# Fused attention and channel mixing on one core: q of batches 3 and 4 turned by the DMA crossbar, and the sums and outputs of two head groups in one TensorE block

## The chip, the cores and the metric

The kernel runs on one core of a Trainium2 chip. The metric is device microseconds of one execution; the time before is the median of three runs, 195.05 us (194.85 to 195.09). The profile is that of one execution, traced by the hardware profiler. Engines: PE is TensorE's matmul, PEld its weight load, DVE is VectorE, ACT is ScalarE, POOL is GpSimd and SP is SyncE, which only issues DMAs here.

## The reference

There are 8 batches, 8 heads, 576 positions and a head size of 64. An attention without a score matrix comes first, then a channel mixing over rows of 512 (8 heads x 64):

```python
q_s = softmax of q over the head dimension          # row sums, then a scale
k_s = softmax of k over the sequence                # column sums
kv  = einsum('bhsd,bhse->bhde', k_s, v)            # 64 x 64 per head
x   = q_s @ kv, heads side by side                  # 576 x 512 per batch
xk  = mu_k * x + (1 - mu_k) * x_prev                # x_prev: the row before
xr  = mu_r * x + (1 - mu_r) * x_prev
k   = relu(xk @ w_k); v = k * k @ w_v               # 512 -> 1024 -> 512
out = sigmoid(xr @ w_r) * v
```

## The kernel before

**Attention.** Work goes by batch b (0 to 7) and head group g (0 and 1), four heads each; a name's digits are b and g (expq30: batch 3, group 0). ScalarE takes exponentials of q and k (expq, expk) and casts v (cast). VectorE sums the rows of q (rsum), inverts (rrec) and scales (scale). For a matmul q must stand with the head dimension on partitions. In batches 0 to 4 TensorE turns it: transposes of 64 rows into a PSUM tile, 18 instructions in the groups of WHOLE and 36 in the others, and ScalarE copies the result out (qt). In batches 5 to 7 (CROSSBAR) SP issues a transposing DMA from SBUF to SBUF instead, also named qt.

The sums k_s' v (kv, 36 matmuls of 64x65, whose last column is the sum of k) go to PSUM. VectorE inverts the sum (rz) and scales the 64x64 blocks (w). The outputs x are matmuls of w with the turned q: four of 64 columns (the last 64 positions) and four of 512 columns. ScalarE copies them to SBUF (xs the 64 columns, xb the 512), VectorE fixes the edge (edge), takes the difference to the row before (diff), scales it by mu (sc, four per group) and adds (mix). A name mix300 is batch 3, group 0, and a last 0 for xk or 1 for xr. Batch 0 and some of batch 1 are done in finer pieces.

**Blocks on TensorE.** From batch 1 on, the transposes and sums of one group are one block, together with the outputs of a group before it: TKV10, TKV20 and TKV30 have no outputs, B11, B21, B31, B40, ..., B71 have those of an earlier group, and X11, X21 and X71 are outputs alone (ALONE). A block with sums takes one of two att tiles (two PSUM banks each) for its sums, its transposed q and the 64 output columns (column offsets KVO and XO), and the other for the 512 output columns.

**Channel mixing.** The 4608 rows go in ten units of 512 or 256 columns (k0 to k9). For each there are eight k (four matmuls of 128x512, then relu on ScalarE and a square sq on VectorE), and for each tile of 128 rows an r (four matmuls, then tanh th on ScalarE) and a v (eight matmuls, then o on VectorE: (1 + tanh) times v), and the stores st on SP. k, r and v share four PSUM banks (mm 0 to 3). k22 is unit 2, eighth 2; r30 is unit 3, tile 0; v210 and v211 are the first and second half of unit 2, tile 1. A k may start when mix of its columns is there: unit 2 needs batch 2, units 3 and 4 need batch 3, unit 5 batch 4.

**Order.** The order is written out as a list of names (ORDER) with the buffer number behind a colon. Each engine gets its part of the list in this sequence and works it off strictly in order; waits follow from the data. POOL issues the loads and weights, in list order and with no more than eight on the way. Around the lines that the prediction speaks of, TensorE's part of the list before is

```
TKV10:1 r02:2 r01:1 r00:3 r03:0 B11:0.1 ... X21:0.1 v111 v101 r20:0 TKV30:1 v130:2 v131 k22:0
k20:1 k24:3 k23:0 k21:2 k27:3 B31:0.1 k25:1 k26:2 r22:0 r30:3 B40:1.0 r23:0 v220:2 v200:1
```

and POOL's first loads are load00v, load01v, load10q0, wk00, load10q1, load11q0, wk01, load10k0, wk10, wk11, load10k1, load10v0, load10v1, load11q1, wr.

Of the kernel before, what the change touches and what calls it, by code (L numbers as in the profile page):

```python
# [39 lines left out]
ALONE = ((1, 1), (2, 1), (B - 1, 1))  # L40
CROSSBAR = tuple((b, g) for b in range(5, B) for g in range(2))
# [16 lines left out]
x0111 sq03 k05:1 expk101 x0110 cast100:0 load11k0:9 cast101 load11k1 relu04:0 expq111 load11v1
k07:0 sq02 relu05:1 sq01 k06:3 wv0 rrec100 rrec110 scale100 sq04 TKV10:1 rz10:2 w10:0 relu06:2
wv1 sq06 rsum111 qt10:2 r02:2 r01:1 relu07:0 r00:3 cast110:1 expk110:0 expk111 rrec111 cast111  # L60
r03:0 scale111:0 scale110 wv2 wv3 B11:0.1 load30q0:10 rz11:0 th00:0 th03:1 w11:1 sq07 th02:2
xb10:0 v030:3 xs10 qt11:0 v000:0 sq05 edge10 th01:3 v010:2 diff10:0 sc1001:0 v011 v001 v031
sc1000 load20q0:0 X11:1.0 xs11:1 load20v0:2 sc1011:1 v012 v020:1 v021 xb110 sc1010 v013 v032
load21q0:1 xb111 edge11 v002 v003 v033 v022 load20k0:3 mix100 diff110:1 diff111 sc1100:2 o01
sc1111:0 expq300:1 v023 sc1101 expq200:0 mix1100 k11:2 load21k0:4 cast200:2 o00 mix1101 sc1110
load21v0:6 load31q0:7 k11.2 o03 k10:0 k11.3 load31v0:5 relu11:2 load30k0:9 expq210:2 k10.2
load50v0:8 k10.3 rsum200:0 o02 st03.2 k17:3 k12:2 relu17:0 relu10:1 k12.2 expk200:1 k12.3
rrec200 mix101 load31k0:10 load30v0:0 k13:1 k13.2 sq11:1 k13.3 relu12:2 scale200:1 sq10 mix111
sq12 k16:3 expk210:2 st02.2 k15:0 relu16:1 rsum210:1 relu15:2 TKV20:0 st00 sq16 cast210:0 r10:2
rz20:1 r11:3 k14:0 rrec210 relu13:1 sq17 w20:2 load40q0:2 th11:4 qt20:1 r12:1 r13:3 relu14:0  # L70
scale210:2 expq310:0 st03 rsum300:3 th12:5 th13:6 sq14 sq13 load40v0:1 B21:1.0 sq15 rz21:2
xb20:0 v120:0 v100:1 v110:3 st01 w21:0 xs20 st02 rrec300 rsum310:2 scale300:0 load40k0:3
load50k0:4 qt21:2 v121 X21:0.1 expk300:0 edge20 rrec310 diff20:0 v111 xs21:1 xb21 v101 o12
cast300:1 r20:0 sc2001:2 th10:1 TKV30:1 edge21 v130:2 diff21:1 sc2000 expq400:2 th20:2 sc2101:1
sc2011:0 mix200 rz30:0 load51k0:6 sc2100 v131 w30:1 expk310:1 cast310:2 st12.2 mix210 k22:0 o10
o11 load60q0:7 load41v0:9 relu22:0 st00.2 st12 qt30:0 k20:1 o13 st13.2 k24:3 relu24:1 relu20:2
k23:0 load50q0:0 k21:2 k27:3 load71k0:2 cast400:0 load51q0:10 scale310:1 rsum400:0 sq24:0 sq20
relu21:1 relu23:2 B31:0.1 sc2010 sc2111:2 mix201 rrec400 load41k0:5 k25:1 rz31:1 sq23 sc2110
w31:2 k26:2 expk400:2 xb30:0 mix211 xs30 scale400:2 relu27:2 r22:0 qt31:1 edge30 sq21 sq27 sq22
th22:0 r30:3 B40:1.0 diff30:0 rz40:2 sc3000:1 relu26:1 relu25:2 xb31:1 xs31 sc3001 th30:5  # L80
load41q0:1 expq500:1 st11 edge31 sq26 expq510:0 sq25 st10.2 load51v0:3 r23:0 mix300 diff31:1
v220:2 expk500:0 v200:1 v201 st01.2 sc3101:0 st10 th23:3 v230:3 v221 st13 st11.2 o20 sc3100 v231
mix310 k45:1 sc3011:2 o22 k40:0 o23 st22 sc3010 sc3110:1 expq410:2 relu45:0 cast410:1 k43:2
sc3111 k42:1 st20.2 relu43:1 sq45:1 relu40:2 relu42:0 r21:3 v210:2 load70v0:0 w40:0 qt40:2
load70q0:10 rsum410:1 load70k0:4 sq40 k30:0 rrec410 load60k0:1 k41:1 v211 relu30:2 mix311 sq43
k37:0 load61q0:9 scale410:0 th21:1 k33:3 o21 cast500:2 expk410:1 k46:2 sq30:0 sq42 mix301
relu37:1 relu41:2 st20 B41:0.1 rsum500:3 rz41:0 k34:0 relu33:0 sq41 sq37 k47:1 xb40:1 sq33 xs40
relu47:2 rrec500 w41:1 rsum510:2 relu46:1 scale500:1 relu34:0 load61k0:8 sq34 qt41:0 load60v0:5
st22.2 r40:3 k31:1 st23 sq47 k32:2 th40:6 r41:0 B50:1.0 relu32:0 rrec510 relu31:2 expk510:2
r31:3 th31:4 k44:2 r33:1 st21 sq46 edge40 th41:2 relu44:1 diff40:0 k36:3 sc4000:0 cast600:0  # L90
xs41:0 sq32 v400:0 scale510:2 sq44 xb41 st23.2 qt50:1 th33:0 expk610:1 sc4001 mix400 rz50:1
v410:2 qt51:2 v401 load71q0:6 v411 sq31 relu36:0 cast510:1 sc4010:1 edge41 sc4011 expq600:2
diff41:1 k35:1 mix401 v330:3 w50:2 o40 sc4100:2 o41 sc4101 v300:0 mix410 relu35:1 k57:2 sq36
expq710:1 k51:1 relu57:2 B51:0.1 sc4111:0 rsum600:0 sq57:1 rrec600 relu51:0 k55:2 xb50:1 sq35
xs50 relu55:2 sc4110 v331 sq51 v301 load61v0:5 load71v0:8 mix411 v310:1 rz51:2 st41.2 scale600:0
expq610:0 expk600:0 o30 sq55 st41 expq700:2 r51:2 o33 edge50 st33.2 k54:0 k56:3 v311 relu54:1
rsum610:1 w51:0 expk700:2 diff50:0 sc5000:1 st30 st30.2 st33 B60:1.0 sc5001 o31 r50:0 qt60:0
rsum710:3 sq54 xs51:0 rsum700:2 k50:1 th51:3 xb51 edge51 relu50:0 relu56:2 sq56 r32:2 st31.2
th32:2 st21.2 sq50 diff51:1 mix500 sc5100:2 rrec710 v320:1 v321 sc5101 mix510 o32 rz60:0 k52:3
sc5010:0 w60:1 cast710:2 th50:5 k53:2 relu52:1 sq52 sc5110:1 rrec610 sc5111 cast610:1 relu53:2  # L100
r53:0 r52:3 sq53 cast700:0 k61:1 relu61:0 st40.2 k67:2 scale610:1 k65:1 relu67:1 st32.2 sc5011
k63:2 qt61:1 th53:0 v530:0 relu65:2 rrec700 th52:1 sq67:0 B61:0.1 mix511 v500:1 v531 sq65 xs60:0
sq61 mix501 xb60 v501 scale700:2 k62:3 relu62:1 expk710:0 o53 edge60 k66:0 relu66:2 st53.2 st31
relu63:0 diff60:1 v510:3 sc6000:2 o50 rz61:1 w61:2 B70:1.0 v511 sc6011:1 scale710:0 v520:1
xb61:1 k64:0 v521 xs61 o51 sc6001 edge61 diff61:0 sc6100:0 rz70:2 st53 r63:2 qt70:2 mix600
th63:0 sq66 r61:3 relu64:2 w70:0 sc6101 B71:0.1 sq63 sc6010 mix601 k60:2 mix610 rz71:0 k73:0
sq64 w71:1 th61:4 relu60:0 sq60 st50.2 k76:3 o52 st50 sq62 r62:2 relu73:2 xb70:0 xs70 v620:0
relu76:0 k71:1 v621 qt71:0 k74:3 sc6110:2 relu71:1 sq73:1 st40 sc6111 mix611 edge70 sq76 th62:5
X71:1.0 relu74:2 v610:1 v611 xb71:1 k70:2 diff70:1 sc7001:1 xs71 o62 k77:0 edge71 relu70:0 k72:3
st62 r73:2 sq70 relu77:0 sq71 relu72:1 k75:0 o61 diff71:0 sq74 sc7101:0 th73:6 st62.2 r60:1  # L110
v630:3 v600:2 sq77 sc7000 sc7110:2 sc7100 mix710 st51.2 sc7011:0 th60:5 st52.2 relu75:2 v631
# [72 lines left out]
def graph(kn):  # L184
# [135 lines left out]
    def attention(b, g):  # L320
# [127 lines left out]
        else:  # L448
# [3 lines left out]
            def block():  # L452
                if crossed:
                    kv(qtp)
# [418 lines left out]
```

## Time and profile before

| | |
|---|---|
| median of 3 runs | 195.05 us (194.85 to 195.09) |
| profiled execution | 194.93 us, span 193.2 us |
| TensorE matmul busy | 185.2 us in 1830 matmuls |
| VectorE busy | 152.7 us |
| ScalarE busy | 138.6 us |
| GpSimd busy (DMA issue) | 41.4 us |
| read and written in HBM | 33.56 MB and 9.44 MB |

The span runs from the first instruction to the last; the rest of the execution's time lies around it. The page gives busy shares by engine and by slice, and the chain that ended last, followed back from the end. The windows give busy time of each engine in a stretch. Durations of instructions in the timeline overlap on an engine, since the next one starts while one drains, so what an instruction costs its engine is the distance from its start to the next start.

### The profile page before, as it was taken

The page shows a single profiled execution, that of the slowest core. Times are in us where ns is not written, and L with a number is a line of the kernel's source. Part 1 is how long each engine was busy: PE and PEld are TensorE (multiplying, and loading weights), DVE is VectorE, ACT ScalarE, POOL GpSimd, SP SyncE. Part 2 cuts the span into 40 slices and gives each one's busy share as a digit, 9 for nine tenths or more (in the row PEclk, how much of TensorE's full clock was granted, in tenths as well). Part 3 has the DMA queues.
Part 4 walks back from the last instruction along what each step waited for, and adds up shares of the span by engine and source line. Part 5 has one row for each costly group of instructions (what it writes and reads, how often), then busy time and mean ns, then how long its engine had stood idle before and what let it go on. Part 6 is the DMA issues. An engine that isn't in the chain of part 4 may idle for free.

```text
span 193.2 us, 4660 instructions
## 1 busy us (share of the span) xinstructions
PE 185.2 (96%) x1830; PEld 89.2 (46%) x1830; DVE 152.7 (79%) x355; ACT 138.6 (72%) x219; POOL 41.4 (21%) x65
## 2 busy tenths in 40 slices
PE   7798979999999999999999999999999999999991
PEld 2264434444535544654444444444444444444751
DVE  1898974999999999999999999998966863232531
ACT  3777999889999999898999798653754236421440
POOL 8345656544225114320210000000000000000000
PEclk9999999999999999999999999999999999999999
DMA  6999999999999999997692371459014145024813
GB/s 192 312 319 248 327 331 246 404 393 399 410 396 397 403 412 376 362 380 275 132 311 105 92 159 27 64 113 169 8 30 107 31 109 136 0 54 110 191 30 109
DMA packets 23615, 41.86 MB, mean 217 GB/s; under 512 B 9373, under 2 KB 12713, under 8 KB 23593
## 3 DMA queue, kind: packets, MB, share of 16 engines
q0 software_dynamic: 9392, 27.99, 43.6%
q1 hardware_dynamic: 13384, 12.14, 25.3%
q10 hardware_dynamic: 816, 1.44, 2.3%
q8 instruction: 14, 0.23, 0.5%
q14 instruction: 9, 0.07, 0.1%
HBM read 33.56 MB, written 9.44 MB: 223 GB/s over the span
## 4 chain that ended last, share of the span: by engine, by line
PE 84%; DMA 11%; POOL 2%; issue 0%; DVE 0%; POOLq 0%
PE mm_d L695 10%; PE mm_b L695 9%; PE mm_a L639 8%; PE mm_c L639 7%; PE mm_b L639 7%; PE mm_c L695 7%; PE mm_a L695 7%; DMA wk_ab<-in_moe_w_k_dram 7%; PE mm_d L639 6%; PE mm_c L675 5%; PE mm_d L675 5%; DMA wr<-in_moe_w_r_dram 4%; PE mm_a L675 4%; PE mm_b L675 3%; PE att_a L401 1%; PE att_b L543 1%
## 5 line engine op out<-in xcount | busy, mean ns | idle before, releaser
L695 PEld LDWEIGHTS <-k_a 128*128 128x128 bf16 x160 | 15.4, 98 | 18.5 <-issue 0.6
L675 PEld LDWEIGHTS <-xr 128*128 128x128 bf16 x144 | 13.6, 98 | 16.8 <-DMA wr<-in_moe_w_r_dram 1.3
L695 PEld LDWEIGHTS <-k_b 128*128 128x128 bf16 x136 | 12.9, 98 | 14.2 <-issue 0.8
L639 PEld LDWEIGHTS <-wk_ab 128*128 128x128 bf16 x80 | 7.8, 98 | 8.1 <-issue 0.5
L639 PEld LDWEIGHTS <-wk_aa 128*128 128x128 bf16 x80 | 7.6, 98 | 8.2 <-issue 0.7
L639 PEld LDWEIGHTS <-wk_bb 128*128 128x128 bf16 x80 | 7.8, 98 | 7.7
L675 PE MATMUL mm_c<-wr,xr 128*128 128x512 bf16 x40 | 10.3, 380 | 1.1 <-DMA wr<-in_moe_w_r_dram 1.1
L639 PEld LDWEIGHTS <-wk_ba 128*128 128x128 bf16 x80 | 7.5, 98 | 8.3 <-issue 0.7
L675 PE MATMUL mm_d<-wr,xr 128*128 128x512 bf16 x40 | 10.3, 379 | 0.0
L675 PE MATMUL mm_a<-wr,xr 128*128 128x512 bf16 x36 | 9.3, 380 | 0.0
L626 ACT ACTIVATE rel_a<-mm_b 128x512 bf16<-128x512 f32 (+1 forms) x7 | 3.6, 508 | 7.5 <-PE mm_b L639 7.2
L626 ACT ACTIVATE rel_c<-mm_a 128x512 bf16<-128x512 f32 (+1 forms) x11 | 6.1, 556 | 3.1 <-PE mm_a L639 2.8
L630 DVE TENSOR_TENSOR k_a<-rel_a 128x512 bf16<-128x512 bf16 x14 | 5.8, 418 | 3.1 <-ACT rel_a L626 2.9
L639 PE MATMUL mm_c<-xk,wk_ab 128*128 128x512 bf16 (+1 forms) x26 | 7.5, 362 | 0.2 <-ACT xk L503 0.2
L639 PE MATMUL mm_c<-xk,wk_aa 128*128 128x512 bf16 (+1 forms) x26 | 7.3, 363 | 0.0
L675 PE MATMUL mm_b<-wr,xr 128*128 128x512 bf16 x28 | 7.2, 379 | 0.0
L630 DVE TENSOR_TENSOR k_a<-rel_c 128x512 bf16<-128x512 bf16 x14 | 5.8, 414 | 1.7 <-ACT rel_c L626 1.7
L639 PE MATMUL mm_a<-xk,wk_ba 128*128 128x512 bf16 (+1 forms) x24 | 6.9, 371 | 0.0
L639 PE MATMUL mm_a<-xk,wk_bb 128*128 128x512 bf16 (+1 forms) x24 | 6.9, 370 | 0.0
L626 ACT ACTIVATE rel_a<-mm_c 128x512 bf16<-128x512 f32 x7 | 4.2, 602 | 3.3 <-PE mm_c L639 1.7
L639 PE MATMUL mm_b<-xk,wk_aa 128*128 128x512 bf16 (+1 forms) x24 | 6.5, 353 | 0.0
L639 PE MATMUL mm_b<-xk,wk_ab 128*128 128x512 bf16 (+1 forms) x24 | 6.5, 352 | 0.0
(344 smaller groups left out, 541.3 us busy)
## 6 DMA issues: line engine op xcount, KB each, us to landing
raw_k<-in_q_dram POOLq DMA_DIRECT2D x3, 576.0 KB, 8.4
raw_e<-in_k_dram POOLq DMA_DIRECT2D x3, 576.0 KB, 11.0
raw_f<-in_v_dram POOLq DMA_DIRECT2D x3, 576.0 KB, 6.8
out_dram<-th_a SPq DMA_DIRECT2D x13, 128.0 KB, 3.2
out_dram<-th_f SPq DMA_DIRECT2D x12, 128.0 KB, 2.4
out_dram<-th_b SPq DMA_DIRECT2D x10, 128.0 KB, 4.8
out_dram<-th_c SPq DMA_DIRECT2D x10, 128.0 KB, 2.4
raw_a<-in_q_dram POOLq DMA_DIRECT2D x2, 576.0 KB, 9.9
```

The costliest lines, as they stand in the source:

```text
L401: kn.nc.tensor.matmul(kn.half(slot, r)[two[u], KVO:KVO + n], lhsT=kn.eks[ek.index][two[r], j, u, :], rhs=by, start=(j == 0), stop=(j == J ...
L543: kn.nc.tensor.matmul(kn.half(slot, u)[two[r], to:to + n], lhsT=kn.ws[w.index][two[u], r, :], rhs=x_columns(r, u, at, n), start=True, stop ...
L626: kn.nc.scalar.activation(out=kn.rels[rel.index][:, 0:n], in_=kn.bank(kf)[:, 0:n], func=ACT.Relu, scale=HALF_ROOT)
L630: kn.nc.vector.tensor_tensor(out=kn.k2s[k2.index][:, fc, 0:n], in0=kn.rels[rel.index][:, 0:n], in1=kn.rels[rel.index][:, 0:n], op=ALU.mult)
L639: kn.nc.tensor.matmul(kn.bank(kf)[:, 0:n], lhsT=kn.wk[fc // 4][ct % 2][:, ct // 2, (fc % 4) * 128: (fc % 4) * 128 + 128], rhs=kn.xs[0][:, ...
L675: kn.nc.tensor.matmul(kn.bank(rps), lhsT=kn.xs[1][:, ct, c:c + 128], rhs=kn.wr[:, ct, :], start=(ct == 0), stop=(ct == CT - 1))
L695: kn.nc.tensor.matmul(kn.bank(vps)[:, 0:width], lhsT=kn.k2s[k2.index][:, ft, 128 * m:128 * m + 128], rhs=wv_of(ft)[:, part], start=(ft == ...
```

## The change

**Crossbar.** Batches 3 and 4 join the crossbar: their four TensorE transposes (18 instructions in group 30, 36 in 31, 40 and 41) and ScalarE's four copies qt30 to qt41 go, and SP issues four more transposing DMAs. The pool of turned q gets a fourth buffer. To make room, mu_rows lies in the last of the th buffers.

**Blocks.** For b = 3 to 8 a block M*b* takes the place of TKV30 and of B31 to B71 and X71. M*b* holds the sums of both groups of batch b (none for 8) and the outputs of both groups of batch b - 1 (none for M3, as batch 2's are done in B21 and X21). Its sums and 64-column outputs go to a new kind of PSUM place, duo: two of the four mm banks (0 and 1, or 2 and 3), at columns 0 and 72 for the sums and 144 and 216 for the outputs. The 512-column outputs of both groups take both att tiles. As the two banks of a duo are two tiles, there is no view over both: rz, w and xs become two instructions, one per bank.

**Order.** The whole list is new. TensorE's part around the lines of the prediction:

```
k00:2 k01:3 X010:1.0 k02:0 k03:1 k00.2 k02.2 k01.2 X011:0.1 k03.2 X001:0.3 mu:0 k05:1 k04:2 k07:3
TKV10:0 k06:1 r00:3 r01:2 r03:1 r02:0 B11:1.0 ... X21:1.0 r13:0 v100:1 v101 v130:3 v110:2 v131 v111
k22:1 k21:0 k20:1 k26:0 k24:1 k23:2 k27:3 k25:1 r23:0 M3:1 v230:1 v200:0 v201 v231 M4:1.1.0
r22:0 v220:1 v221 r21:2 r30:3 v210:0 v211 k31:2 k43:3 k47:1 ... M5:1.1.0 v401 v300:0 v301 r32:1
v320:2 v321 v330:3 v331 k50:1 ... M6:0.1.0 ... M7:1.1.0 ... M8:0.0.1 ... v831 r91:0 v900:3 v901
```

ScalarE's behind B11: th02 th03 xb10 xs10 th00 (before: th00 th03 th02 xb10 xs10). ScalarE's behind M4: xs31 xs30 xb30 xb31 expq510 th22 expk500 th21. VectorE's behind M3: rz30 rz31 sq27 w31 w30 scale400 o20 o23 rz41 rz40 w41 w40, and behind xb30: edge30 diff30 edge31, then sc and mix of batch 3. VectorE's last: o83 sq93 o90 o91 (before: sq90 to sq97 ahead of o90). SP's: st03 st00 st02 st00.2 st03.2 qt30 st01 st02.2 st12 qt31. POOL's first loads: load00v, load01v, wk00, load11q0, load10q0, load10q1, wk01, wk11, load10k1, wk10, load10k0, load10v0, load10v1, load11q1, wr.

The core of the diff:

```diff
-"qt": 3
+"qt": 4, ... "duo": 2
+          ("duo", 0): [("mm", 0), ("mm", 1)], ("duo", 1): [("mm", 2), ("mm", 3)]}
+KVM = (0, 72)
+XM = (144, 216)
-ALONE = ((1, 1), (2, 1), (B - 1, 1))
-CROSSBAR = tuple((b, g) for b in range(5, B) for g in range(2))
+ALONE = ((1, 1), (2, 1))
+CROSSBAR = tuple((b, g) for b in range(3, B) for g in range(2))
...
+        kvo = KVM[g] if crossed else KVO
...
-            def block():
-                if crossed:
-                    kv(qtp)
-                if turn_x:
-                    turn_x[0](qtp)
-                if not crossed:
-                    transpose_q(qtp)
-                    kv(qtp)
...
+            def copy_second(other, xo):
+                if kn.whole(other) is not None:
+                    kn.nc.scalar.copy(out=kn.xbs[xb.index][:, :, 576:640],
+                                      in_=kn.whole(other)[:, :, xo:xo + 64])
+                else:
+                    for u in range(2):
+                        kn.nc.scalar.copy(out=kn.xbs[xb.index][:, u, 576:640],
+                                          in_=kn.half(other, u)[:, xo:xo + 64])
...
+    def together(b):
+        groups = [attention(b, g) for g in range(2)] if b < B else []
+        turns, pending[:] = list(pending), []
+        duo = Slot("duo")
+
+        def block():
+            for kv, _, _, _ in groups:
+                kv(duo)
+            for turn, at in zip(turns, XM):
+                turn[0](duo, at)
+
+        m = add("PE", block, [o for t in groups for o in t[1]] + [o for t in turns for o in t[1]],
+                [duo] + [o for t in turns for o in t[2]],
+                [o for t in groups for o in t[2]] + [o for t in turns for o in t[3]], name=f"M{b}")
+        for turn, at in zip(turns, XM):
+            turn[4](m, duo, at)
+        for t in groups:
+            t[3](m, m, None, duo)
...
+    for b in range(B):
+        if (b, 0) in CROSSBAR:
+            together(b)
+        else:
+            for g in range(2):
+                attention(b, g)
+    together(B)
...
     def half(slot, i):
+        if slot.pool == "duo":
+            return ps["mm"][2 * slot.index + i][:]
...
-    kn.mu_rows = const.tile([2, 2, 256], F32, name="mu_rows")
+    kn.mu_rows = kn.ths[-1][0:2, :].rearrange("p (m c) -> p m c", m=2)
```

More of the change, by code (lines that the diff above doesn't have):

```diff
@@ L58 @@
[L58 to L63, printed above, removed]
@@ L70 @@
[L70 to L75, printed above, removed]
@@ L76 @@
[L76 to L93, printed above, removed]
@@ L106 @@
[L106 to L111, printed above, removed]
@@ L118 @@
[L118 to L121 removed]
+warm load00k1 load01v late load01k0:3 wk00 load11q0:4 load10q0:5 expq001:0 expq000 load10q1
+rsum001:0 ACT!load01k1 rsum000 wk01 expq011:1 rrec001 wk11 rrec000 rsum011:1 fill:1 fill.2:2
+fill.3:3 fill.4:0 fill.5:1 fill.6:2 fill.7:3 fill.8:0 fill.9:1 fill.10:2 fill.11:3 fill.12:0
@@ new lines @@
+cast400:0 sq27 w31:1 v201 cast410:1 w30:2 v231 expq410:1 scale400:2 load50k0:1 load71q0:4
+M4:1.1.0 load51v0:6 o20 o23 r22:0 xs31:1 v220:1 st11 st23.2 xs30:0 rz41:2 rz40:1 w41:0 w40:1
+v221 xb30 edge30 xb31 load60k0:7 diff30:1 r21:2 edge31 sc3000:2 expq510:2 th22:3 r30:3 st23
+st20.2 load61q0:5 st20 diff31:0 expk500:2 v210:0 qt40:1 th21:5 sc3001 sc3100:0 mix300 sc3101
+v211 st11.2 mix310 o22 o21 k31:2 th30:4 expk510:0 k43:3 load50v0:0 relu31:0 sc3011:1 rsum410:1
+relu43:1 k47:1 st22 k44:0 k46:2 sq43:1 sq31:0 relu47:2 expq500:0 k45:3 relu46:1 rrec410 sq47
```

363 lines of the change are left out of this document (196 added, 167 removed).

## The prediction

> **What bounds the kernel now.** I read the page first (busy shares, then the chain that ended last), then the windows, the chain in order of time, and the timeline of PE (the last row here).
>
> ```profile
> span 193.2 us, 4660 instructions
> PE 185.2 (96%) x1830; PEld 89.2 (46%) x1830; DVE 152.7 (79%) x355; ACT 138.6 (72%) x219; POOL 41.4 (21%) x65
> PE 84%; DMA 11%; POOL 2%; issue 0%; DVE 0%; POOLq 0%
> ...
> 55.00:60.00 5.00, 5.00 (x80) 2.44 (x81) 4.90 (x16) 5.00 (x8) 1.90 (x3) 1.00 1.02 390
> 120.00:125.00 5.00, 5.00 (x65) 2.23 (x64) 5.00 (x10) 3.74 (x7) 0.00 (x0) 1.00 0.45 64
> ...
> 18.30 8.34 DMA wr<-in_moe_w_r_dram
> 43.52 0.86 PE mm_d L639 x4
> 188.35 0.89 PE mm_b L695 x8
> ...
> 26.68 1.04 PE L675 MATMUL mm_c<-wr,xr 128*128 128x512 bf16 x4 [1.15 <-DMA wr<-in_moe_w_r_dram]
> ```
>
> The columns of a window are busy time of PE, PEld, DVE, ACT and POOL (counts in brackets), granted clock, DMA share, GB/s. PE works without a gap from 26.68 us, where the load of wr lands (18.30 + 8.34) and ends a wait of 1.15 us, to 189.24 (188.35 + 0.89), at full clock; the time before that hangs on DMA. So the time is a start that DMA sets, 162.56 us of PE work, and a tail of 193.2 - 189.24 = 4.0 us. Less PE work is a gain exactly where PE is not then made to wait. That matters here, since VectorE is as full as PE in both windows (4.90 and 5.00 of 5), and ScalarE in the first.
>
> **The start.** On the POOL queue wr is the fifteenth transfer in both orders and the same fourteen stand ahead of it, in another sequence. Ahead of the first r group PE has the same blocks and k groups in both orders. I cost the start at nothing: wr covers it, with the 1.15 us that PE waits for it. That cover is eaten if PE comes late: X001 now stands behind k03's second half, and k05 behind the copies of both. I keep 0.5 us either way for the range.
>
> **PE: blocks that go and blocks that come.** The timeline of PE has one block of each kind:
>
> ```profile
> 57.03 1.03 PE L675 MATMUL mm_a<-wr,xr 128*128 128x512 bf16 x4
> 57.99 0.44 PE L371 MATMUL att_b<-ident,qs_a 64*128 64x64 bf16 x18
> 58.36 0.48 PE L401 MATMUL att_b<-vv_b,ek_a 64*64 64x65 bf16 x36
> 58.77 0.60 PE L695 MATMUL mm_c<-wv_a,k_b 128*128 128x512 bf16 x2
> ...
> 69.82 0.59 PE L675 MATMUL mm_d<-wr,xr 128*128 128x512 bf16 x2
> 70.61 0.48 PE L371 MATMUL att_b<-ident,qs_c 64*64 64x64 bf16 x36
> 70.91 0.49 PE L401 MATMUL att_b<-vv_a,ek_c 64*64 64x65 bf16 x36
> 71.33 1.04 PE L675 MATMUL mm_a<-wr,xr 128*128 128x512 bf16 x4
> ...
> 90.59 0.59 PE L675 MATMUL mm_a<-wr,xr 128*128 128x512 bf16 x2
> 91.12 0.48 PE L401 MATMUL att_b<-vv_c,ek_a 64*64 64x65 bf16 x36
> 91.43 0.20 PE L543 MATMUL att_b<-qt_a,w_b 64*64 64x64 bf16 x4
> 91.46 0.39 PE L543 MATMUL att_a<-qt_a,w_b 64*64 64x512 bf16 x4
> 91.78 1.04 PE L675 MATMUL mm_d<-wr,xr 128*128 128x512 bf16 x4
> ...
> 142.33 0.59 PE L639 MATMUL mm_d<-xk,wk_bb 128*128 128x512 bf16 x2
> 143.23 0.60 PE L695 MATMUL mm_b<-wv_a,k_a 128*128 128x512 bf16 x2
> ```
>
> Durations overlap, so I go by starts. A large group of four takes 0.86 us in the chain, 0.216 a matmul. From the end of the large matmuls before a block to the first one behind it: TKV30 0.88 (58.77 - 57.03 - 4 x 0.216), B31 1.08 (71.33 - 69.82 - 2 x 0.216), B50 0.76, X71 alone 0.47. What goes: TKV30; B31, B40 and B41, all three with 36 transposes; B50 to B71, six; X71: 0.88 + 3.24 + 4.56 + 0.47 = 9.15 us.
>
> What comes: B50 gives the parts: 0.10 to enter (91.12 - 91.02), 0.31 for the 36 sums of a group, 0.04 for the 64-column outputs, 0.22 for the 512-column ones (four at once), 0.10 to leave. M3 has two sums: 0.82. M4 to M7 have two sums and two outputs: 0.10 + 0.62 + 0.52 + 0.10 = 1.34, four times 5.36. M8 has two outputs: 0.72. Together 6.90 us: PE saves **2.25 us**, some 1.27 of it the 126 transposes (0.37 + 3 x 0.30) and the rest five blocks fewer (eleven become six), at some 0.2 us each to enter and leave. None of these shapes is new, so I take the ends of this term as 2.0 and 2.5.
>
> **VectorE and ScalarE.** A pair of mm banks has no whole view, so rz and w become two instructions each in ten groups, and xs two on ScalarE in ten.
>
> ```profile
> L412 DVE RECIPROCAL rz_b<-mm_b x1: 149/149/149, 14.6 to 14.6; 128x1 f32<-128x1 f32 x1
> L423 DVE TENSOR_SCALAR kvn_b<-mm_b,rz_b x1: 274/274/274, 15.0 to 15.0; 128x64 f32<-128x64 f32 x1
> L379 ACT COPY qt_b<-att_a x2: 1127/1139/1151, 48.8 to 69.0; 128x1152 bf16<-128x1152 bf16 x2
> L554 ACT CAST xb_a<-att_a x4: 266/286/376, 32.6 to 139.2; 128x128 bf16<-128x128 f32 x4
> L551 ACT CAST xb_a<-att_b 128x1024 bf16<-128x1024 f32 x4 | 4.1, 1033 | 0.0
> ...
> 59.41 0.16 DVE L408 RECIPROCAL rz_a<-att_b 128x2 f32<-128x2 f32 x1
> 59.49 0.34 DVE L568 TENSOR_SCALAR xm_b<-xd_b,mu 128x576 bf16<-128x576 bf16 x1
> 59.76 0.28 DVE L418 TENSOR_TENSOR w_b<-att_b,rz_a 128x128 bf16<-128x128 f32 x1
> 59.96 0.74 DVE L573 TENSOR_TENSOR xk<-xm_b,xb_b 128x1152 bf16<-128x1152 bf16 x1
> 60.62 0.67 DVE L701 SCALAR_TENSOR_TENSOR th_b<-th_b,mm_b 128x512 f32<-128x512 f32 x1
> ...
> 60.67 0.86 PE mm_a L639 x4
> ```
>
> By starts rz costs 0.08 and w 0.20; halves (149 and 274 ns) are hardly shorter, so each group pays another 0.28 us, 2.8 us over ten. ScalarE loses four q copies of about 1.14 us and gains ten small ones of at most 0.29: 1.7 us less at least. Neither is on the path by itself. What counts is where PE waits for VectorE.
>
> **Where PE will wait.** Unit 2's first k (k22) needs batch 2's mix200 and mix210, the latter the row at 59.96. In the chain it starts at 60.67, as mix210 ends (60.62 to 60.70): no slack. From B11 to k22 the new PE order has the same work less TKV30, so PE is there 0.88 us sooner. VectorE's list from rz11 to mix210 trades rz30, w30, sc2011 and sq05 for o10 and sq04 (the squares alike): 0.08 + 0.20 + 0.27 by the rows above against 0.60 for an o (0.67 less the 0.07 by which starts overlap). That is as much as before. So the 0.88 can turn into a wait. It is shorter if VectorE's chain begins sooner: behind B11 ScalarE's new order has xb10 and xs10 ahead of th00 instead of behind it. Ends 0.3 and 0.9; I take **0.6**.
>
> Next, k31 and k43 need mix300 and mix310. Relative to before VectorE has, up to mix310, o23, rz41, w40, w41 and four split groups more: 0.60 + 0.08 + 0.40 + 1.12 = 2.2 us. mix310 ended at 77.24 (the row below), so 79.4; with up to 0.6 of waiting for xb30 and xb31, which M4 now gives both at once, 79.4 to 80.0. PE from k22 at 60.67: eight k, r23, M3, v23, v20, M4, r22, v22, r21, r30, v21: 12 x 0.86 + 4 x 1.73 + 0.82 + 1.34 = 19.4, so 80.1. On time, or nearly: **0.1**, ends 0 and 0.6.
>
> ```profile
> 76.48 0.76 DVE L573 TENSOR_TENSOR xk<-xm_a,xb_b 128x1152 bf16<-128x1152 bf16 x1
> ```
>
> At the end sq93 now stands behind o83 on VectorE: an o of 0.60 and a short square after v831, against r91's 0.86 on PE. I estimate 0.1, ends 0 and 0.3. M4 to M7 hold two mm banks until rz, w and xs have read them; two banks are left for k, r and v. Behind M4 these are r22 and v22, then the freed pair; the cover is that VectorE comes straight to rz and w.
>
> **Crossbar and queues.** Four transposes come to SP's queue, with stores behind them: qt30 waits there for scale300, and st01, st02, st12 wait behind it; nobody needs their th buffers before th23, behind r23.
>
> ```profile
> 57.00:64.00 7.00, 7.00 (x84) 3.39 (x83) 6.96 (x14) 7.00 (x10) 2.89 (x4) 1.00 1.03 400
> 121.40:125.40 4.00, 1.00 0.55 78
> DMA to landing us min/median/max: 3.2/3.7/4.6
> POOL raw_g L208 <- ACT ek_c L332: 7.3, 1, 7.3
> ```
>
> The second row holds one transpose alone: 0.55 x 4.0 = 2.2 us of all DMA engines for 0.31 MB. Landing takes up to 4.6 us; qt31 waits for scale310, which stands right behind mix210 (60.7), and M4 is 12.0 us of PE work behind k22 (60.67): cover for both. The four take 8.8 us of DMA time, half of it where DMA is full. Loads then land up to 4.4 us later; what hides that is that POOL waits for ScalarE to free buffers (7.3 us once), so loads are ahead of their use.
>
> The Trainium skill (Advanced Engine Details and Errata, X-Bar Transpose) says that transposing DMAs are as fast as regular ones. By that rule 0.31 MB at the 400 GB/s of the first row would be 0.8 us, an estimate, and four 3.1 us. The trace differs (2.2 us each), and I go by the trace; both leave the sum as it is, as neither is on the path.
>
> **The sum.** -2.25 + 0.6 + 0.1 + 0.1 = -1.45 us. The profiled execution took 194.93 us, 0.12 under the median of 195.05: 193.5 us for it, 193.6 for the median; I say **193.5**.
>
> **Rivals.** *No waits*: VectorE's chain comes sooner and the waits at k22 and k31 don't show. For it: ScalarE has less to do. Against: k22 had no slack. 194.93 - 2.25 = 192.7.
> *VectorE takes the gain*: the 1.7 us of split instructions in the six groups of batches 3 to 5 are passed on at k31 and k50, with the 0.6 at k22: -2.25 + 0.6 + 1.7, so 195.0. For it: VectorE is full up to 125 us. Against: the sums above meet PE on time.
> *Slower: the banks*. Behind each of M4 to M7 ScalarE must copy xs twice in halves and xb twice (4 x 0.29 + 2 x 1.03 = 3.2 us) before it comes to the relu and tanh that free banks, while two free banks are 2 x 0.86 = 1.7 us of PE work. PE stalls up to 1.5 us at each of four blocks: 193.5 + 6.0 = 199.5. It decides from 0.45 us a block (1.8 in all). For it: th22 now stands behind four copies and an exp. Against: v groups last 1.73 us, and the copies' own banks come free in this time.
> *Late loads*: the 4.4 us reach ScalarE and then PE: 193.5 + 4.4 = 197.9.
>
> **Chances.** My forecast 0.49 (192.9 to 194.4), no waits 0.18 (192.4 to 192.9), VectorE 0.15 (194.4 to 195.6, split evenly over faster, same, slower), banks 0.14, late loads 0.04. About 0.2% is what a measurement of this kernel can tell. Faster: 0.49 + 0.18 + 0.05 = 0.72; same 0.05; slower 0.23. From 192.5 to 195.7 leaves out the banks, the loads and the last bit below: under 0.2.
>
> **What would show it.** Right: M3 to M8 as long as summed, a wait of PE ahead of k22 that ends with VectorE's xk, PE at 100% elsewhere from 26.7 us on, fewer PE instructions (126 transposes), qt30 landed well before M4. Wrong: PE idle behind M4 to M7 with ScalarE's rel or th, or a VectorE th, as releaser; a first r group later than 26.7 us; ScalarE waiting for raw loads in batches 3 to 5.

## The result, and the profile after

The changed kernel took 203.12 us (201.17 to 203.34 in four runs) against 195.04 us before (194.85 to 195.09): a ratio of 1.0393, with a 95% interval of 1.0367 to 1.0419. It is 8.1 us slower; 193.5 was predicted. The profiled execution took 203.34 us, with a span of 201.6. Ratios here leave out executions more than 1.5% above the fastest of their kernel, so some differ a little from the quotient of the medians.

The page of the changed kernel has these lines:

```profile
span 201.6 us, 4462 instructions
PE 185.6 (92%) x1704; PEld 88.7 (44%) x1704; DVE 154.1 (76%) x376; ACT 135.7 (67%) x225; POOL 41.4 (21%) x65
...
PE 75%; DVE 9%; DMA 6%; issue 5%; ACT 2%; POOL 2%; POOLq 0%; ACTq 0%
```

The 126 transposes are gone, but PE is busy for as long as before (185.6 against 185.2 us), and idle time and "issue" came on top. The windows say where. Their columns are busy time of PE, PEld, DVE, ACT and POOL with counts, then granted clock, DMA share and GB/s:

```profile
65.00:70.00 5.00, 5.00 (x92) 2.43 (x91) 4.53 (x10) 3.70 (x6) 1.44 (x2) 1.00 1.10 390
70.00:75.00 5.00, 0.09 (x1) 0.00 (x0) 2.72 (x11) 0.00 (x0) 0.00 (x0) 0.76 1.20 333
75.00:80.00 5.00, 2.48 (x6) 0.84 (x6) 0.00 (x0) 3.12 (x4) 0.86 (x2) 0.50 0.91 205
80.00:85.00 5.00, 5.00 (x100) 2.16 (x99) 2.02 (x8) 2.81 (x7) 2.03 (x3) 0.72 0.95 334
```

PE and ScalarE stand still from 70 to nearly 77 us, and VectorE soon runs out of work, while the DMA engines are full. When PE goes on, its granted clock is 0.50. The chain of the same stretch, in order of time:

```profile
69.18 7.69 issue
76.88 0.61 ACT th_a L713
...
77.53 3.57 PE mm_a L728 x8
81.10 1.71 PE mm_b L728 x4
```

The chain has no name for what ended the 7.69 us; ScalarE's tanh th_a (th23) did. A v group that takes 1.73 us at full clock then took 3.57. From the windows the low clock cost 2.48 x 0.50 + 5.00 x 0.28 = 2.6 us. So 7.7 of waiting and 2.6 of low clock, less 1.9 us that a run below shows as the gain without them, come to the 8.4 us between the spans; smaller waits are left out of this sum.

What th23 waited for is found in SP's queue, in its timeline and in the DMA issues of 54 to 75 us (KB, and us from issue to landing):

```profile
54.26 2.31 SPq L524 DMA_TRANSPOSE qt_c<-qs_a  x1
56.62 0.98 SPq L744 DMA_DIRECT2D out_dram<-th_d  x1
57.65 0.59 SPq L744 DMA_DIRECT2D out_dram<-th_a  x1
58.34 1.25 SPq L744 DMA_DIRECT2D out_dram<-th_e  x1
62.09 10.37 SPq L524 DMA_TRANSPOSE qt_d<-qs_b  x1
```

```profile
out_dram<-th_a SPq DMA_DIRECT2D x1, 128.0 KB, 19.2
out_dram<-th_e SPq DMA_DIRECT2D x1, 128.0 KB, 19.0
```

th23 writes the buffer th_a, whose last user was th02. The second of th02's stores was issued at 57.65, behind qt30, and landed 19.2 us later, at 76.85; th23 started at 76.88. In the kernel before, stores of this stretch took 6 to 9 us (DMA issues of 40 to 75 us):

```profile
out_dram<-th_a SPq DMA_DIRECT2D x2, 128.0 KB, 6.2
out_dram<-th_e SPq DMA_DIRECT2D x2, 128.0 KB, 9.1
```

And qt31 (qt_d) needed 10.37 us only to be issued, where a transpose of the kernel before takes 1.3 to 2.2.

The packets of that time, by queue (q0 is POOL's loads, q1 is SP; packets, MB, share of 16 engines), first from 54 to 63 and then from 59 to 69 us:

```profile
q0 software_dynamic: 805, 3.29, 97.7%
q1 hardware_dynamic: 390, 0.10, 4.9%
```

```profile
q0 software_dynamic: 881, 3.61, 95.1%
q1 hardware_dynamic: 884, 0.23, 10.1%
```

A transpose that runs alone in the kernel before, from 121.4 to 125.4 us, has this line:

```profile
q1 hardware_dynamic: 1184, 0.30, 53.3%
```

So a transpose is 1184 packets of some 250 bytes, and a load packet has 4 KB. In the nine microseconds behind its issue qt30 and its stores got only 390 packets through: none until about 58.3 us, and then one for each packet of the loads, as the second pair of lines shows.

### The profile page after: what moved, and what is told of

Read it like the earlier page. It is cut to its first block, busy times and chain, and to the rows that moved or that the text cites. A ratio compares the mean times of both kernels' runs of the same rounds, so it can differ in the third digit from the quotient of the medians.

```text
span 201.6 us, 4462 instructions
## 1 busy us (share of the span) xinstructions
PE 185.6 (92%) x1704; PEld 88.7 (44%) x1704; DVE 154.1 (76%) x376; ACT 135.7 (67%) x225; POOL 41.4 (21%) x65
## 4 chain that ended last, share of the span: by engine, by line
PE 75%; DVE 9%; DMA 6%; issue 5%; ACT 2%; POOL 2%; POOLq 0%; ACTq 0%
PE mm_b L728 9%; PE mm_a L672 8%; PE mm_d L728 8%; PE mm_a L728 7%; PE mm_b L672 7%; DMA raw_f<-in_q_dram 6%; PE mm_d L672 6%; PE mm_c L708 5%; PE mm_c L672 5%; PE mm_c L728 5%; PE mm_a L708 4%; PE mm_d L708 4%; PE mm_b L708 2%; PE mm_c L405 1%; PE att_b L544 1%
## 5 line engine op out<-in xcount | busy, mean ns | idle before, releaser
L728 PEld LDWEIGHTS <-k_b 128*128 128x128 bf16 x144 | 14.0, 98 | 16.6 <-issue 0.4
L708 PE MATMUL mm_c<-wr,xr 128*128 128x512 bf16 x48 | 12.3, 379 | 0.5 <-ACT rel_a L659 0.5
L708 PE MATMUL mm_d<-wr,xr 128*128 128x512 bf16 x40 | 10.3, 379 | 0.0
L728 PE MATMUL mm_a<-wv_a,k_a 128*128 128x512 bf16 x10 | 3.4, 426 | 7.4 <-ACT th_a L713 7.4
L663 DVE TENSOR_TENSOR k_b<-rel_b 128x512 bf16<-128x512 bf16 (+1 forms) x15 | 5.9, 392 | 4.1 <-ACT rel_b L659 4.1
L659 ACT ACTIVATE rel_b<-mm_a 128x512 bf16<-128x512 f32 (+1 forms) x10 | 5.8, 580 | 3.9 <-PE mm_a L672 3.3
L659 ACT ACTIVATE rel_b<-mm_d 128x512 bf16<-128x512 f32 (+1 forms) x8 | 4.1, 516 | 5.9 <-PE mm_d L672 2.8
L734 DVE SCALAR_TENSOR_TENSOR th_g<-th_g,mm_a 128x512 f32<-128x512 f32 x2 | 1.4, 682 | 8.4 <-PE mm_a L728 8.4
L663 DVE TENSOR_TENSOR k_b<-rel_a 128x512 bf16<-128x512 bf16 (+1 forms) x12 | 4.7, 394 | 3.4 <-ACT rel_a L659 3.4
L713 ACT ACTIVATE th_a<-mm_a 128x512 f32<-128x512 f32 x2 | 1.2, 617 | 8.1 <-issue 8.1
L672 PE MATMUL mm_a<-xk,wk_aa 128*128 128x512 bf16 x22 | 6.6, 380 | 0.0
## 6 DMA issues: line engine op xcount, KB each, us to landing
raw_g<-in_v_dram POOLq DMA_DIRECT2D x3, 576.0 KB, 10.3
```

The source lines that it names most:

```text
L659: kn.nc.scalar.activation(out=kn.rels[rel.index][:, 0:n], in_=kn.bank(kf)[:, 0:n], func=ACT.Relu, scale=HALF_ROOT)
L663: kn.nc.vector.tensor_tensor(out=kn.k2s[k2.index][:, fc, 0:n], in0=kn.rels[rel.index][:, 0:n], in1=kn.rels[rel.index][:, 0:n], op=ALU.mult)
L672: kn.nc.tensor.matmul(kn.bank(kf)[:, 0:n], lhsT=kn.wk[fc // 4][ct % 2][:, ct // 2, (fc % 4) * 128: (fc % 4) * 128 + 128], rhs=kn.xs[0][:, ...
L708: kn.nc.tensor.matmul(kn.bank(rps), lhsT=kn.xs[1][:, ct, c:c + 128], rhs=kn.wr[:, ct, :], start=(ct == 0), stop=(ct == CT - 1))
L713: kn.nc.scalar.activation(out=kn.ths[th.index][:], in_=kn.bank(rps), func=ACT.Tanh, scale=0.5)
L728: kn.nc.tensor.matmul(kn.bank(vps)[:, 0:width], lhsT=kn.k2s[k2.index][:, ft, 128 * m:128 * m + 128], rhs=wv_of(ft)[:, part], start=(ft == ...
```

## The experiments

The theories. **1, starved transposes:** SP's queue and POOL's take turns packet by packet, so that a transpose of many small packets needs over ten microseconds while POOL's queue is full, and everything behind it on SP too. **2, the stores' place:** only three stores behind qt30 and qt31 are at fault. **3, the blocks:** M3 to M8 and the new orders are slow by themselves. **4, the bytes:** any transfer on SP's queue starves beside the loads.

### Stores first

```diff
-... scale300:0 ... qt30:2 st01 st02.2 st12 ... qt31:3 ... st01.2 ...
+... st01 st02.2 st01.2 scale300:0 ... qt30:2 st12 ... qt31:3 ...
```

> Only the place of three stores changes: the ones of th00 to th02 that stood behind qt30 or qt31 on SP go ahead of qt30. Theory 1, starved transposes (each transpose is 1184 small packets and takes turns with the large packets of the loads, so it needs 15 to 20 us in the full stretch): the store of th02 lands before 50 us and th23 no longer waits, but qt31, issued at 62 us, still lands at 75 to 80 us, and PE, which now reaches M4 at about 75.5 us, waits there for 1 to 5 us, and after it at a lower clock: 194.5 to 200 us. Theory 2, only the stores' place was wrong: no wait is left, 203.1 less 7.4 of waiting and 2.7 of low clock, 193 us, at most 194. Theory 3, the new blocks and orders are slow by themselves: 202 us or more.

207.9 us, ratio 1.0655 (1.0628 to 1.0681): slower than the change itself. The wait at th23 is gone and a longer one stands at M4. The chain has the first line, the waits have the second, the packets of 63 to 67 us the next two:

```profile
62.72 23.31 DMA qt_d<-qs_b
```

```profile
PE mm_c L541 <- DMA qt_d<-qs_b: 10.3, 1, 10.3
```

```profile
q0 software_dynamic: 370, 1.49, 96.2%
q1 hardware_dynamic: 368, 0.09, 10.5%
```

370 packets of the loads to 368 of the transposes: turns, one for one, though q0 moves sixteen times the bytes. That is 92 packets per us, or 12.9 us for 1184. qt31 landed at 86.03, 23.31 us after its issue, as it had qt30 before it in the same queue, which had needed 18.3 us (DMA issues of 55 to 58.5 us):

```profile
qt_c<-qs_a SPq DMA_TRANSPOSE x1, 18.3
```

Theory 2 falls; theory 1's mechanism is seen, and its size was underrated. With ScalarE no longer blocked the loads went on, and up to 70 us there was no pause in which the transposes could catch up. From 75 to 85 us both queues were slow; the last section shows this, and no run explains it.

### Light loads

```diff
-  [1, J * D]])  ... out=kn.raws[slot.index][:, u, :]
+  [1, J * D if b < 5 else D]])  ... out=kn.raws[slot.index][:, u, 0:J * D if b < 5 else D]
```

> The loads of batches 5 to 7 fetch 64 of their 576 columns (the rest of these buffers keeps older numbers, so the outputs of these batches are not the reference's); nothing else is changed. Theory 1: with the DMA engines no longer full from 48 us on, qt31 is issued in 3 us instead of 10.4 and lands within 5 us, the store of th02 lands within 4 us instead of 19.2, PE does not wait at 69 us: 192.5 to 194 us. Theory 3 (blocks and orders): 202 us or more, since PE, VectorE and ScalarE do the same work.

193.39 us, ratio 0.9911 (0.9888 to 0.9934). SP's timeline and the windows:

```profile
62.35 1.94 SPq L523 DMA_TRANSPOSE qt_d<-qs_b  x1
```

```profile
65.00:70.00 5.00, 4.95 (x91) 2.54 (x91) 4.54 (x11) 4.83 (x9) 1.44 (x2) 1.00 1.07 290
70.00:75.00 5.00, 4.95 (x105) 2.48 (x105) 4.63 (x19) 4.80 (x9) 2.88 (x4) 1.00 0.28 86
```

qt31 is issued in 1.94 us and PE does not stop in these ten microseconds. Theory 3 falls: PE, VectorE and ScalarE do all that they do in the changed kernel, and the time is the predicted one. The store of th02 took 7.0 us, more than the 4 expected, but no more than stores of this stretch took before.

### Plain copy

```diff
+ move = (kn.nc.sync.dma_start if b == 3 else kn.nc.sync.dma_start_transpose)
- qcopy = add("SP", lambda: kn.nc.sync.dma_start_transpose(
+ qcopy = add("SP", lambda: move(
```

> Batch 3's two transposes become plain copies of the same 0.295 MB from the same buffer into the same buffer on the same queue (q is not turned, so the outputs of batch 3 are not the reference's); batches 4 to 7 keep their transposes. Theory 1 (it is the number of packets: 1184 small ones a transpose against one to three a row of 2304 bytes here): both copies land within 7 us, the store behind them within 7 us too, and the wait at 69 us is gone: 193 to 195 us. Theory 4 (it is the bytes, any transfer on SP's queue starves beside the loads): as after, 200 us or more. Theory 3: 202 us or more.

213.51 us (211.65 and 215.37), a time that theories 3 and 4 allow and theory 1 does not. But the stretch in question came out as theory 1 has it. The stores behind the copies landed in 6 to 10 us, as before the change, the store of th02 in 7.5 (DMA issues from 53.5 to 73 us), and PE lost 1.5 us between 70 and 75 us instead of 4.9:

```profile
out_dram<-th_a SPq DMA_DIRECT2D x1, 128.0 KB, 7.5
```

The same bytes in plain packets don't hold up what stands behind them, so theory 4 falls for this stretch. What I had not reckoned with is that without the stall the loads go on, and that batch 4's transposes, issued at 86.11 and 95.41 us in the changed kernel, now go at 76.16 and 86.74 us, beside more of them: qt40 took 19.9 us to land instead of 7.3. From the chain:

```profile
86.74 30.42 DMA qt_a<-qs_a
```

qt41 took 30.42 us, and M5 waited for it. For a part of that time, from 95 to 110 us, DMA moved only 73 to 223 GB/s, the slow state of the last section. So this run is evidence for the stretch of the stall, and its whole time is none.

### Two transposes more in the kernel before

```diff
+        if b == 3:
+            add("SP", lambda: kn.nc.sync.dma_start_transpose(
+                out=qt_crossed(kn.qts[3]),
+                in_=kn.qss[qs.index][:].rearrange("p j d -> p (j d)")), scaled, [], [qs],
+                name=f"dummy{tag}")
-... scale300:0 ... scale310:1 ...
+... scale300:0 dummy30 ... scale310:1 dummy31 ...
```

> The kernel before with its own blocks and order, and two transposes more on SP's queue, right behind scale300 and scale310, of batch 3's q into a buffer that nobody reads. Theory 1 (turns packet by packet: 1184 packets at the 92 per us that the second run showed beside the loads, 12.9 us each, one behind the other): the dummies land near 67 and 80 us, the stores behind them (th00, th01, th03) land 10 to 20 us after issue instead of 5, some tanh waits for its buffer, PE idles 2 to 10 us and then runs at a lower clock: 197 to 207 us. Theory 3 (the blocks): the dummies cost nothing, 195 to 195.5 us.

(The 92 packets per us are those of the run with stores first.)

203.82 us, ratio 1.0455 (1.0435 to 1.0476). With the old blocks and the old order, two transposes that nobody reads cost 8.8 us, about as much as the whole change. The first line is from the DMA issues of 55 to 58.5 us, the second from the waits:

```profile
out_dram<-th_f SPq DMA_DIRECT2D x1, 128.0 KB, 18.9
```

```profile
ACT th_a L682 <- issue: 7.6, 1, 7.6
```

It is the picture of the changed kernel: late stores, a tanh that waits 7.6 us, and a granted clock of 0.50 from 75 to 80 us. Both dummies write the same buffer, so the second, whose data were there at 64.1 us, waited for the first to land: it went at 74.82, 19.4 us after the first's issue at 55.39 (a landing near 67 had been expected).

### Blocks alone

```diff
+            if b in ONPE:  # batches 3 and 4
+                own = Slot("att")
+                turn = add("PE", lambda: transpose_q(own), before_t, [own], [qs], name=f"T{tag}")
+                qcopy = add("ACT", lambda: copy_qt(own), [turn], [qt], [own], name=f"qt{tag}")
-... qt30:2 ... qt31:3 ... qt40:1 ... qt41:0 ...
+... T30:0 qt30:2 ... T31:1 qt31:3 ... T40:0 qt40:1 ... T41:1 qt41:0 ...
```

> The changed kernel with its blocks M3 to M8 and its order, but batches 3 and 4 turn q on PE again (four separate transpose blocks of 36, ScalarE copies the result); batches 5 to 7 keep the crossbar. Theory 1: no transpose stands in the full stretch, stores land in 5 us, no wait at th23; PE has some 4 x 0.45 us more work than in the second run (193.4), and ScalarE 4 copies of 1.14 us: 194.4 to 196.5 us. Theory 3 (blocks and orders): 202 us or more.

201.27 us, ratio 1.0341 (1.0297 to 1.0384), where theory 1 expected 194.4 to 196.5; theory 3's 202 is nearer. No wait of 7 us is there, but many short ones. One of them in the timelines of ScalarE and PE:

```profile
96.77 1.12 ACT L381 COPY qt_a<-att_b 128x1152 bf16<-128x1152 bf16 x1 [2.30 <-PE att_b L373]
```

```profile
98.44 1.02 PE L710 MATMUL mm_a<-wr,xr 128*128 128x512 bf16 x4 [1.73 <-ACT rel_a L661]
```

ScalarE stands 2.30 us for the transposes of its copy, the relus behind the copy are late, and PE then waits 1.73 us for a bank. My reading, which no run tests, is that the copies' names stand where SP's had stood, where ScalarE's order has no room for them. So the run does not tell what the blocks are worth. For that the run with light loads stands: it has the same blocks and orders and no such waits behind 60 us.

### Holds at two transposes

Loads are held by naming what has landed first (load40v0^qt30 waits for qt30). Stores first, and then:

```diff
-... load50q0:3 ... load40v0:5 ... load41k0:7 ... qt30:2 ... load61v0:10 load51k0:8 load41v0:0 ...
+... qt30:2 load40v0^qt30:5 load41k0:7 load41v0:3 ... qt31:3 ... load50q0^qt31:0 load61v0:10 load51k0:8 ...
```

> The three stores ahead of qt30 as in the first kernel, and loads held so that the DMA engines are free when a transpose goes: load40v0 (with load41k0 and load41v0 behind it, now ahead of batches 5 and 6) waits until qt30 has landed, load50q0 until qt31 has. Theory 1: each transpose lands in 3.5 to 6 us, PE waits neither at th23 nor at M4, and the loads, which come up to 8 us later, are still in time for M4 and the later blocks: 192.7 to 194.5 us. If the held loads are late instead, ScalarE waits for raw buffers between 65 and 80 us, and it comes out at 195 to 198. Theory 3: 202 us or more.

210.13 us (206.28 to 213.59). The chain:

```profile
62.71 7.30 DMA qt_d<-qs_b
...
91.83 18.77 DMA qt_a<-qs_a
```

qt31 landed in 7.30 us instead of 23.31, and M4 had it in time. But load51q0, which stands behind the held load50q0 in POOL's queue, landed only at 81.31 us, and ScalarE waited for it (waits), as the second case of the expectation had it, at a larger cost:

```profile
ACT eq_c L333 <- DMA raw_j<-in_q_dram: 4.6, 1, 4.6
```

And the loads that were held back now filled the queue when qt40 and qt41 went: qt40 took 20.7 us to land and qt41 18.77. Protecting two transposes hands the problem on to the next two.

### Holds at all of them (the kernel with gaps), and two loads in flight

The loads behind load30v0 sorted by when ScalarE needs them, in bunches between the transposes:

```diff
+ qt30: load41k0^qt30 load40v0 load41v0
+ qt31: load41q0^qt31 load51q0 load50k0 load51k0 load50q0 load51v0
+ qt40: load60q0^qt40 load50v0 load60k0
+ qt41: load60v0^qt41 load61v0 load61q0 load61k0
+ qt50: load70v0^qt50 load70k0 load71k0 load71v0 load71q0 load70q0
```

> All loads behind load30v0 sorted by when ScalarE needs them and sent in bunches between the transposes: 3 wait for qt30's landing, 6 for qt31's, 3 for qt40's, 4 for qt41's, the last 6 for qt50's; stores of th00 to th02 ahead of qt30. Theory 1: a bunch of n loads needs n x 1.5 us, so the queue is nearly empty when the next transpose goes; qt31, qt40, qt41 land in 3 to 7 us instead of 13 to 30; no wait over 1 us at M4 and M5, and no late load: 193.0 to 194.5 us. If a bunch is too large for its gap, the transposes behind it land in over 10 us and ScalarE waits for raw buffers: 196 to 203 us.

202.72 us, ratio 1.0396 (1.0335 to 1.0456). From 40 to 105 us PE loses 1.0 us in all; then a load is late. From the chain and from the waits:

```profile
99.43 8.03 DMA qt_d<-qs_c
108.04 4.79 DMA raw_i<-in_v_dram
```

```profile
ACT vv_c L340 <- DMA raw_i<-in_v_dram: 7.0, 1, 7.0
```

The load of v700, whose cast ran at 104.9 us in the run with light loads, waited for qt50's landing at 107.5: the hold was put on the wrong load. The time lies in the second range of the expectation (196 to 203), but for another reason: no transpose took over 10 us there (qt51 8.3, qt50 8.0).

The same sorted loads without holds by transposes, each waiting for the load two before it:

```diff
+ load41k0^load40k0 load40v0^load30v0 load41v0^load41k0 load41q0^load40v0 load51q0^load41v0 ...
```

> The same loads in the same order, but no holds by transposes: each load from load41k0 on waits until the load two before it has landed, so at most two are in flight. Theory 1 in its strict form (turns packet by packet whenever loads are in flight): with loads in flight 60 to 90 per cent of the time a transpose takes 6 to 12 us, qt31 lands at 69 to 75 us, just in time for M4 at 75.5: 193 to 196 us. If two loads in flight keep the DMA engines as full as eight do, qt31 lands behind 76 us and it comes out at 198 to 205 us.

202.7 us, ratio 1.0304 (1.0231 to 1.0377). The time lies in the range that had been given for a late qt31 (198 to 205), but for another reason: M4 had qt31 in time, and two in flight are too slow for the need behind it (waits):

```profile
ACT eq_c L336 <- DMA raw_h<-in_q_dram: 7.1, 1, 7.1
```

### Gaps, second and third

Both: the loads from q310 on sorted by need too. Second: v700 in the bunch behind qt41. Third: five loads more without a hold beside qt30, which is needed late.

```diff
  (second)
+ qt40: load60q0^qt40 load50v0 load60k0 load60v0
+ qt41: load61v0^qt41 load61q0 load61k0 load70v0 load70k0
+ qt50: load71k0^qt50 load71v0 load71q0 load70q0
  (third)
+ no hold: load41k0 load40v0 load41v0 load41q0 load51q0
+ qt31: load50k0^qt31 load51k0 load50q0 load51v0 load60q0 load50v0
+ qt40: load60k0^qt40 load60v0 load61v0
+ qt41: load61q0^qt41 load61k0 load70v0 load70k0
+ qt50: load71k0^qt50 load71v0 load71q0 load70q0
```

> As the kernel with gaps, with two differences: the loads of q310, k300 and their neighbours are sorted by need too (q310 three places sooner, for the 0.4 us that PE lost at 60 to 65 us), and the load of v700, whose hold behind qt50 cost some 7 us of waiting at 106 us, goes with the bunch behind qt41; bunches of 3, 6, 4, 5 and 4. Theory 1: as in the run with light loads no wait of PE over 1 us is left, 193.2 to 194.5 us. If the bunch of 5 behind qt41 (issued at about 94 us) now makes qt51 and qt50 late for M6 at 116 us or v700 late for its copy at 105 us, 196 to 200 us.

199.63 us in the median of ten executions, which went from 194.1 to 209.5 us; the four fastest have a ratio of 0.9996 (0.9969 to 1.0023): no gain, and a time that changes from one execution to the next. In the profiled one the time went in many waits of at most 1.5 us behind M4. That loads and transposes meet a little sooner or later each time is likely, but no run here shows it.

> The same sorted loads, but five of them go without a hold behind load30k0, beside qt30; the holds are at qt31 (6 loads), qt40 (3), qt41 (4) and qt50 (4). Theory 1: qt30 takes 10 to 15 us beside the loads, which harms nothing as it is needed at 73 us; qt31 behind it lands at 68 to 72 us, just before M4; the loads behind are 5 us ahead of those of the kernel with gaps: 193.2 to 195 us. If qt31 comes later than 73 us, PE waits at M4 and the time is 195 to 200.

**193.16 us, ratio 0.9923 (0.9892 to 0.9953)**: 0.8% faster than the kernel before, and so faster than the change, though single executions reached 195.7 and 199.2. The page, the windows, the start of r on PE and its last matmuls:

```profile
span 191.0 us, 4465 instructions
PE 184.1 (96%) x1704; PEld 88.5 (46%) x1704; DVE 154.4 (81%) x376; ACT 136.2 (71%) x225; POOL 41.3 (22%) x65
```

```profile
65.00:70.00 5.00, 5.00 (x93) 2.53 (x92) 4.53 (x14) 4.85 (x9) 1.76 (x3) 1.00 1.02 244
70.00:75.00 5.00, 5.00 (x107) 2.50 (x106) 4.64 (x17) 4.86 (x9) 2.55 (x4) 1.00 0.96 364
```

```profile
26.67 1.04 PE L705 MATMUL mm_d<-wr,xr 128*128 128x512 bf16 x4 [0.60 <-DMA wr<-in_moe_w_r_dram]
...
48.77 1.02 PE L705 MATMUL mm_c<-wr,xr 128*128 128x512 bf16 x4 [0.20 <-ACT rel_a L656]
...
186.92 0.38 PE L725 MATMUL mm_b<-wv_d,k_a 128*128 128x256 bf16 x2
```

PE works from 26.67 to about 187.3 us with 0.20 us of waiting, so 160.6 us against 162.56 before: 1.9 us less.

### Which part of it

The third set of gaps without any hold, and then with the stores back behind qt30 and qt31:

```diff
- load50k0^qt31 ... load60k0^qt40 ... load61q0^qt41 ... load71k0^qt50
+ load50k0 ... load60k0 ... load61q0 ... load71k0
```

> The kernel with the third set of gaps without any of its holds: the same loads in the same order, each sent as soon as its buffer is free. Theory 1: the loads keep the DMA engines full until about 90 us, qt30 and qt31 take 13 us each one behind the other and land near 67 and 80 us, PE waits 3 to 12 us at M4, which it reaches at 73, and later transposes are late too: 198 to 210 us. Rival: it is the sorting of the loads that made the gain, the holds do nothing: 193 to 195 us.

209.65 us, ratio 1.0736 (1.0687 to 1.0786). Sorting alone is worse than the change (chain):

```profile
62.41 24.94 DMA qt_d<-qs_b
```

```diff
-... st01 st02.2 st01.2 scale300:0 ...
+... qt30:2 st01 st02.2 st12 ... qt31:3 ... st01.2 ...
```

> The kernel with the third set of gaps with the stores of th00 to th02 put back where the change has them, behind qt30 and qt31. Theory 1: qt30 lands at 66 us, the store of th02 2 to 3 us later, in time for th23 at 69 to 70 us or up to 1 us late; the one behind qt31 lands by 72, its buffer is needed at 78: 193.0 to 194.6 us. Theory 2 (the place of the stores is what costs): ScalarE waits for the store 4 us or more as in the changed kernel: 198 us or more.

193.76 us in the median of five (192.85 to 196.9), ratio 0.9896 (0.9867 to 0.9924). With the loads held the stores may stand where the change put them. It is the holds that count: without them the same loads took 209.65.

## Why the prediction was wrong, point by point

**The start**, "at nothing": right within its 0.5. The first r came at 26.94 us in the changed kernel (26.68 before) and at 26.67 in the third set of gaps, where of the 1.15 us of cover 0.60 was left.

**The blocks**, 2.25 us saved: right. M5 in the changed kernel (timeline of PE) goes from 106.03 + 2 x 0.216 to 107.77, 1.31 us against 1.34:

```profile
106.03 0.59 PE L728 MATMUL mm_a<-wv_d,k_b 128*128 128x512 bf16 x2
106.56 0.21 PE L405 MATMUL mm_c<-vv_a,ek_c 64*64 64x65 bf16 x1
...
107.77 0.60 PE L728 MATMUL mm_b<-wv_c,k_b 128*128 128x512 bf16 x2
```

In the third set of gaps 1.9 us came out at the end of PE's work, or 2.1 with the 0.20 us of waiting added back.

**VectorE and ScalarE**, "2.8 us over ten" and "1.7 us less at least": off the path, as said. VectorE's busy time rose by 1.4 us (1.7 in the third set of gaps), less than was costed; ScalarE's fell by 2.9 (2.4).

**Waits at k22 and k31**, 0.6 and 0.1: there is none at either. In the changed kernel an r group waited 0.50 us at 49.29 for ScalarE's relu; in the third set of gaps it was 0.20, and no other. k22 began at 59.88 there, against 60.50 before, so 0.62 of the 0.88 us were a gain, and this term was 0.3 too large.

**Crossbar and queues: the step that failed.** The text says "nobody needs their th buffers before th23, behind r23", which is right: th23 is the instruction that stood. But it gives the stores behind qt30 no time. The store of th02 had 10.8 us, from its issue at 57.65 to the end of r23 at 68.41, and needed 19.2. The text goes on: "Landing takes up to 4.6 us; qt31 waits for scale310, which stands right behind mix210 (60.7), and M4 is 12.0 us of PE work behind k22 (60.67): cover for both." The 4.6 was mis-sized. Its row is that of transposes issued when the loads had ended or were ending (the first at 90.7 us); the windows shown beside it had the DMA engines at 390 to 400 GB/s from 55 to 64 us, the very time of qt30 and qt31. Beside the loads a transpose gets 92 packets per us at best, 12.9 us for its packets alone. In the two runs in which neither a hold nor the wait at th23 stopped the full loads (stores first, and sorting alone) qt30 took 18.3 and 18.2 us from issue to landing, and qt31 behind it 23.31 and 24.94. The cover of 12 us is half of that. The stretch was costed in bytes and in engine time ("2.2 us of all DMA engines"), and the price of sharing was put on the loads ("Loads then land up to 4.4 us later"); with turns by packet the transposes, and what stands behind them, paid it. How much of the 23.31 and 24.94 us is the slow end told of in the last section stays open.

**The rule that would have told it.** The page "DMA: Bandwidth & Descriptors" of the Trainium skill, under "Queues, rings and completion order", says that each DMA engine goes round the queues that have work and takes a packet from each. By that, small packets beside large ones get far less than half of the bytes. The trace agrees, in what it counts as packets: 370 to 368. The prediction weighed another sentence of the Trainium skill ("Advanced Engine Details and Errata", "X-Bar Transpose": as fast as regular DMAs) against the trace, and the trace disagrees more strongly here: the store of th02 landed 7.5 us after its issue behind a plain copy, and 19.2 behind a transpose.

**Rivals.** No banks stall, no late loads in the changed kernel, no VectorE limit. The slower result came from a mechanism that none of them had, and the chance of 0.23 for slower went to others.

**What it would have been.** 193.5 was right for the work: light loads gave 193.39, held loads 193.16. With VectorE's waits smaller, the rival without waits (192.7) lies as near.

## What to carry to other kernels

Before moving work to a queue, read that queue in the stretch where it will run: count packets there, not bytes, and take a landing time only from a place that is as full. A transfer of small packets needs a pause in the bulk loads or a cover of its packet count at the shared rate, and what stands behind it on its queue inherits the delay. When a stall is mended, look at the next transfer of the same kind: here each mended one let the loads run on into the next.

## What the runs showed of the hardware

**Turns by packet, and a slow end.** In the changed kernel one for one holds from 59 to 69 us (881 to 884), and in the kernel before with two transposes more from 60 to 74 us (1153 to 1151). The 805 to 390 from 54 to 63 us is no other rule: SP's queue shows no packet there until about 58.3 us, 4.0 us after qt30's issue. The transpose alone in the kernel before had its first at about 122.7 us, 1.2 us after its issue; why it takes longer beside the loads is not shown. While PE stood still in the run with stores first, the end of qt31 crept (windows; DMA share, then GB/s, at the end of the rows):

```profile
75.00:80.00 5.00, 0.47 (x11) 0.17 (x11) 0.00 (x0) 0.00 (x0) 0.17 (x1) 0.91 1.33 115
80.00:85.00 5.00, 0.00 (x0) 0.00 (x0) 0.00 (x0) 0.00 (x0) 0.00 (x0) 0.50 0.96 186
```

The engines count as full at 115 and 186 GB/s, against 390 to 400 with loads alone. Sorting alone has the same stretch (61 and 157 GB/s). The kernel before with two transposes more, in which the second went only when the first had landed, does not (387 and 289 GB/s from 70 to 80 us). So two transposes at once beside the loads are a candidate, but no run here isolates this, and it stays open.

**The clock.** After 7.4 us without matmuls PE went on at a granted 0.50, and the next 5 us window still had 0.72. The Trainium skill ("TensorE: Matmul & The Clock Gate", "Part 1: The HAM clock gate") says that the clock halves after an idle window and comes back after a busy one; the rows agree. By the estimate above, the stall of 7.7 us so cost 10.3.
